# Four products ahead of a transpose, a constant column in a softmax, and new due times in a hand-planned kernel

## The chip, the core and the metric

The kernel runs on one core of one Trainium2 chip. The metric is the device time of one execution in microseconds (us); the times given are medians of a few executions. TensorE multiplies matrices, VectorE (DVE) and ScalarE (ACT) work elementwise and read its results from PSUM, GpSimd (POOL) works elementwise on SBUF, and SyncE (SP) issues the loads and stores.

## The reference, cut to what matters

Three stages follow each other: local and summary attention over 2 x 768 tokens with 8 heads of 64, a gated pair of products, and a second one with a clipped gate. All is float32, the weights arrive as float64.

```python
k_sum = k.reshape(B, H, nb, block, D).max(axis=3)       # block 32
v_sum = v.reshape(B, H, nb, block, D).mean(axis=3)
scores_all = concat([where(|i - j| < 16, q k^T / 8, -1e9), q k_sum^T / 8 + log(32)])
a = exp(scores_all - max(scores_all))
a = a / (sum(a) + 1e-09)
x = a @ concat([v, v_sum])
h = ((x @ w1) * (x @ w2)) @ w3 @ w_out                  # first block
g = (h @ w_in); g = g * clip(g + 3, 0, 6) / 6
out = g @ w_out2                                        # second block
```

## The kernel before

**Arithmetic.** Large products run with each operand split in a high and a low float32r part, and three products of 128 x 128 by 128 x 512 per term (PASSES, L338; the matmul is L347). The weights' 64-bit values are turned into float32 by hand (`to_f32`, L252: two ACT steps or an ACT and a DVE step, then a DVE step), then split by `to_hi_lo` (L298: ACT rounds the high part at L301, POOL or DVE subtracts at L304). `LO_DVE` lists the numbers of those conversions in `convert` whose subtraction goes to DVE instead of POOL; `convert` is called 40 times.

**Attention.** Twelve pairs of query tiles of 64 run in turn. `probabilities` (L450) makes the scores of both tiles of a pair (x = 0, 1; L483, plain float32 products on quarters of the array) into banks 6 and 7 of PSUM, scales and masks them on DVE into `sc` (L493), takes the maximum (DVE, L507), subtracts it (POOL, L509), exponentiates (ACT, L510), sums, adds 1e-9 and inverts (DVE, L513 to L515), and multiplies (POOL, L519). `attend` (L521) transposes the probabilities on TensorE (L529, four per x, x = 0 into bank 6, x = 1 into bank 7), copies them to `pt` (L536 on ACT for x = 0, L534 on DVE for x = 1), and multiplies by the values (L544). The order is scores of pair 0, scores of pair 1, transposes of pair 0, and so on. `con` holds the masks (480 columns) and an identity (128). Block sums and maxima come first: `first_k` (L384, three loads of 512 KB and a maximum each, L364), `first_v` (L392, the same with sums, L400), and `vsum_rows` (L421), which transposes the sums through bank 7 and copies them with ACT (L431).

**W'.** Beside the first four pairs, TensorE forms the product of two weights, `wprime` (L657), in 192 products; then come the blocks `ab` and `acc1` of the first stage, and from L900 on the second stage.

**The order.** Nothing is queued by hand. Every operation is entered in `Graph` with an engine, an estimated duration, a due time, what it reads and what it writes. `schedule` (L95) goes back from the users: an operation's due time is the smallest of its users' due times less its own duration and a latency; only TensorE operations bring a due time of their own:

```python
due = [o[2] if o[0] == "pe" else self.LAST for o in self.ops]
...
due[i] = min(due[i], due[u] - self.ops[i][1] - self.LAT.get(e, 40))
```

It then plays the engines forward, each taking of its ready operations the one due first, and the instructions are emitted in that planned order, so each engine's queue has it. The constants at L157 to L172 (DUE_..., LO_DVE, HOLD, OUT_AT and others) are the due times and options that the plan starts from. The two operations of a pair's transposes are entered as

```python
for x in range(2):
    g.op("pe", 480, due + 7 * us, lambda x=x: trans(x), [("s", i2, x), "con"], [("bank", bk[x])])
    ...
    g.op("dve" if x else "act", 690 if x else 600, due + 7.5 * us, fn, [("bank", bk[x])], [("pt", x)])
```

Of the kernel before, what the change touches and what calls it, by code (L numbers as in the profile page):

```python
# [63 lines left out]
class Graph:  # L64
# [7 lines left out]
    LAST = 1e9  # L72

    def __init__(self):
        self.ops = []
        self.writer, self.readers = {}, {}

    def op(self, eng, ns, due, fn, reads=(), writes=(), lock=False, slack=0, begin=0):
# [75 lines left out]

DUE_W = ((77.78, -6.43), (102.28, 1.95))  # L157
DUE_K, DUE_V, DUE_ROWS = 121.82, -109.4, 7.92
DUE_Q = (307.31, 41.78)
V_AT = 1  # L160
LO_DVE = [2, 9, 15, 16, 17, 18, 22, 26, 28, 29, 30, 31, 32, 36, 38, 42, 44, 45, 47]
L3_ACT = [2, 3, 4, 5, 6, 7, 8, 10, 11, 12, 15, 17, 18, 20, 22, 23, 24]
DUE_FF = 30.71
AHEAD, BEHIND = -16.03, -118.65
SUMS_AT, SUMS_DUE = 3, 5.0
POOL_MAX = ()
HOLD = 3512.7
SUMS_LATER = 22839.1
OUT_LATER = 31254.19
IN_AT = (8, 12)  # L170
LAST_ORDER = (0, 1, 4, 5, 2, 3, 6, 7)
OUT_AT, OUT_STEP = 174.13, 5.88  # L172


def build(tc, qd, kw, vw, kt, vt, consts, wp_in, w12_in, w2_in, out):
# [30 lines left out]
    kall = [att.tile([P, NPAIR, KS], F32, name=f"kall{i}") for i in range(2)]  # L206
    vall = [att.tile([P, DM], F32, name=f"vall{i}") for i in range(4)]
    qst = [att.tile([P, 2, NPAIR, QT], F32, name=f"qst{i}") for i in range(2)]
    sc = [att.tile([P, 2, NPAIR, NK], F32, name=f"sc{i}") for i in range(2)]
    pt = [att.tile([P, NPAIR * P], F32, name=f"pt{i}") for i in range(2)]  # L210
    st = [att.tile([P, 3, 2 * NPAIR], F32, name=f"st{i}") for i in range(2)]
    con = att.tile([P, 4 * NK + P], F32, name="con")
# [143 lines left out]

    load(0, lambda: con, consts, P * (4 * NK + P) * 4, ["con"])
    g.op("pool", 60, 0, lambda: nc.gpsimd.memset(three, 3.0), (), ["three"])


    def max32(due, x, c, reads):
# [88 lines left out]
    def probabilities(u, due, bk):  # L450
        i2, uu = u % 2, u % PPB
        ki, si, sti, qs = kall[i2], sc[i2], st[i2], qst[i2]
        vi = [2 * i2, 2 * i2 + 1]
        load(due - 5 * us, lambda: qs, qd[u], P * 2048, [("qs", i2)])
        near = u < PPK
        if near:
            lo = u * 2 * QT
            from_k = ["ksum"] + [
                ("kres", c) for c in range(3)
                if c * S // 3 + (WIN if c else 0) < lo + KW and lo < (c + 1) * S // 3 + WIN * (1 + (c == 2))]  # L460
        else:
            load(due - 5 * us, lambda: ki[:, :, NSUM : NSUM + KW], kw[u], P * KW * 16, [("kw", i2)])
            from_k = [("kw", i2), ("ks", i2, 0), ("ks", i2, KS - NSUM)]
        for h in range(2):
            rows = slice(0, NWIN) if h else slice(NSUM, NK)
            load(due - 4 * us, lambda h=h, rows=rows: vall[vi[h]][rows, :], vw[2 * u + h], NWIN * 2048, [("vw", vi[h])])

        def parts(x):
            if not near:
                lo = x * (KS - NK)  # L470
                return [(0, ki[:, :, lo : lo + NK])]
            lo = (2 * u + x) * QT
            return [(0 if x else NSUM, kres[:, :, lo : lo + NWIN]), (NWIN if x else 0, ksum)]

        def scores():
            for p in range(NPAIR):
                for n in range(2 if near else 1):
                    for x in range(2):
                        c, keys = parts(x)[n]
                        for h in range(2):  # L480
                            pr, o = slice(h * D, (h + 1) * D), (h + x) % 2 * D
                            rhs = keys[pr, p, :]
                            nc.tensor.matmul(  # L483
                                out=bank[bk[x]][o : o + D, p * NK + c : p * NK + c + rhs.shape[-1]],
                                lhsT=qs[pr, x, p, :], rhs=rhs, start=True, stop=True,
                            )

        g.op("pe", 1500 if near else 1100, due, scores, from_k + [("qs", i2)], [("bank", b) for b in bk])
        for x in range(2):
            m = (0 if uu == 0 else 1) if x == 0 else (3 if uu == PPB - 1 else 2)  # L490
            g.op(
                "dve", 660, due + 1 * us,
                lambda x=x, m=m: nc.vector.scalar_tensor_tensor(  # L493
                    out=si[:, x], in0=bank[bk[x]][:, 0 : NPAIR * NK].rearrange("p (a n) -> p a n", a=NPAIR),
                    scalar=SCALE, in1=con[:, m * NK : (m + 1) * NK].unsqueeze(1).to_broadcast((P, NPAIR, NK)),
                    op0=ALU.mult, op1=ALU.add,
                ), [("bank", bk[x]), "con"], [("s", i2, x)],
            )
        s8 = si.rearrange("p x a n -> p (x a) n")
        s1 = si.rearrange("p x a n -> p (x a n)")  # L500
        skeys = [("s", i2, 0), ("s", i2, 1)]

        def wide(k):
            return sti[:, k, :].unsqueeze(2).to_broadcast((P, 2 * NPAIR, NK))

        g.op("dve", 1160, due + 2 * us,
             lambda: nc.vector.tensor_reduce(out=sti[:, 0, :], in_=s8, op=ALU.max, axis=AX.X), skeys, [("st", i2)])  # L507
        g.op("pool", 2000, due + 3 * us,
             lambda: nc.gpsimd.tensor_tensor(out=s8, in0=s8, in1=wide(0), op=ALU.subtract), [("st", i2)], skeys)  # L509
        g.op("act", 1020, due + 4 * us, lambda: nc.scalar.activation(out=s1, in_=s1, func=AF.Exp), [], skeys)  # L510

        def inv():
            nc.vector.tensor_reduce(out=sti[:, 2, :], in_=s8, op=ALU.add, axis=AX.X)  # L513
            nc.vector.tensor_scalar(out=sti[:, 0, :], in0=sti[:, 2, :], scalar1=1e-9, scalar2=None, op0=ALU.add)
            nc.vector.reciprocal(out=sti[:, 1, :], in_=sti[:, 0, :])  # L515

        g.op("dve", 1560, due + 5 * us, inv, skeys, [("st", i2)])
        g.op("pool", 2000, due + 5.5 * us,
             lambda: nc.gpsimd.tensor_tensor(out=s8, in0=s8, in1=wide(1), op=ALU.mult), [("st", i2)], skeys)  # L519

    def attend(u, due, b0, b1):  # L521
        i2 = u % 2
        j, col = u // PPK, (u % PPK) * 2 * QT
        s0 = A_X + NPAIR * j
        si, vi, bk = sc[i2], [2 * i2, 2 * i2 + 1], (b0, b1)

        def trans(x):
            for p in range(NPAIR):
                nc.tensor.transpose(bank[bk[x]][0:NK, p * P : (p + 1) * P], si[:, x, p, :], ident)  # L529

        for x in range(2):
            g.op("pe", 480, due + 7 * us, lambda x=x: trans(x), [("s", i2, x), "con"], [("bank", bk[x])])
            if x:
                fn = lambda: nc.vector.tensor_copy(pt[1][0:NK, :], bank[bk[1]][0:NK, :])  # L534
            else:
                fn = lambda: nc.scalar.activation(out=pt[0][0:NK, :], in_=bank[bk[0]][0:NK, :], func=AF.Copy)  # L536
            g.op("dve" if x else "act", 690 if x else 600, due + 7.5 * us, fn, [("bank", bk[x])], [("pt", x)])

        def pv():
            for p in range(NPAIR):  # L540
                for x in range(2):
                    for h in range(2):
                        o = p * P + (h + x) % 2 * D
                        nc.tensor.matmul(  # L544
                            out=bank[b0][h * D : (h + 1) * D, p * P + x * QT : p * P + (x + 1) * QT],
                            lhsT=vall[vi[x]][0:NK, (2 * p + h) * D : (2 * p + h + 1) * D],
                            rhs=pt[x][0:NK, o : o + QT], start=True, stop=True,
                        )

        g.op("pe", 1100, due + 8 * us, pv, [("pt", x) for x in range(2)] + [(n, v) for n in ("vw", "vs") for v in vi],  # L550
             [("bank", b0)])
        xb = bank[b0].rearrange("p (a n) -> p a n", a=NPAIR)
        xh = ar[:, s0 : s0 + NPAIR, 0, col : col + 2 * QT]
        xl = ar[:, s0 : s0 + NPAIR, 1, col : col + 2 * QT]
        keys = [("t", s0 + p, h, col) for p in range(NPAIR) for h in range(2)]
        whole = [k for p in range(NPAIR) for k in both(s0 + p)]
        g.op("act", 600, due + 9 * us, lambda: nc.scalar.activation(out=xh, in_=xb, func=AF.Copy),
             [("bank", b0)] + whole, [k for k in keys if k[2] == 0])
        g.op(
            "dve", 690, due + 9.5 * us,  # L560
            lambda: nc.vector.tensor_tensor(out=xl, in0=xb, in1=xh.bitcast(F32), op=ALU.subtract),
            [("bank", b0)] + whole + [k for k in keys if k[2] == 0], [k for k in keys if k[2] == 1],
        )
# [117 lines left out]
    with tc.manual_schedule():  # L681
# [334 lines left out]
        for n, store, i, hh, bks, start in LAST:  # L1016
# [30 lines left out]
            for m in range(2):  # L1047
# [18 lines left out]
                elif n == 3:  # L1066
                    pair_out(due, 1, m, bks[m], 2 + m)
        for _, i in g.schedule():
            g.ops[i][3]()
        for cm in reversed(pools):  # L1070
            cm.__exit__(None, None, None)
# [71 lines left out]
```

## Time and profile before

| | before |
|---|---|
| median of 3 runs | 557.11 us |
| the runs | 555.17, 557.11, 557.39 us |
| the profiled execution, its own time | 555.27 us |
| its span on the core | 553.5 us |
| TensorE busy | 526.9 us |
| DVE busy | 375.7 us |
| ACT busy | 303.5 us |
| POOL busy | 289.2 us |

The span is the stretch from the first to the last instruction on the core; the 1.8 us around it belong to the execution's own time. Busy time alone doesn't tell what sets the end: TensorE's idle time, what ended it, and the chain of work that ended last do. Times in the rows below are counted from the start of the span.

### The profile page before, as it was taken

To read this page: it belongs to the slowest core of one execution; us is meant where nothing else is said; L and a number is where in the kernel's file an instruction comes from. 1 tells how busy PE (TensorE), PEld (TensorE's weight loads), DVE (VectorE), ACT (ScalarE), POOL (GpSimd) and SP (SyncE) were. 2 spreads that over 40 slices of the span, in tenths; PEclk is the share of its full clock that TensorE was granted. 3 is DMA by queue.
4 is the path that set the end of the run, shared out by engine and by line. 5 is a ranking of instruction groups with operands and counts; after the bars stand their busy time and mean duration, and the time that the engine had idled before them with its cause. 6 is when DMAs were issued, how large, how long until landed. Compare 5 with 4: busy or idle time off the path is not lost.

```text
span 553.5 us, 8514 instructions
## 1 busy us (share of the span) xinstructions
PE 526.9 (95%) x3112; PEld 431.4 (78%) x3112; DVE 375.7 (68%) x460; ACT 303.5 (55%) x517; POOL 289.2 (52%) x239
## 2 busy tenths in 40 slices
PE   0399999999999999999999999999999999999997
PEld 0388788888788888888888888888888887888875
DVE  5889978578463447777553866577775569689941
ACT  0879876484232446564545786655663456734630
POOL 0668454673221334374728665875785563644630
PEclk9789999999999999999999999999999999999999
DMA  8999678662241368633347576475444679877631
GB/s 318 363 364 336 197 245 261 187 195 62 65 123 53 121 215 270 218 115 115 114 157 229 222 247 209 156 263 172 150 174 142 209 264 366 294 256 231 190 103 75
DMA packets 54513, 111.32 MB, mean 201 GB/s; under 512 B 4792, under 2 KB 26296, under 8 KB 54472
## 3 DMA queue, kind: packets, MB, share of 16 engines
q1 hardware_dynamic: 54472, 110.79, 59.9%
q8 instruction: 24, 0.39, 0.3%
q14 instruction: 17, 0.14, 0.1%
HBM read 84.26 MB, written 26.21 MB: 200 GB/s over the span
## 4 chain that ended last, share of the span: by engine, by line
PE 91%; DMA 4%; DVE 1%; SPq 1%; POOL 1%; issue 0%; ACT 0%; ACTq 0%; DVEq 0%
PE bank L347 84%; PE bank L544 2%; PE bank L483 2%; PE bank L529 2%; DMA con<-in_con_dram 2%; DMA ws<-arena 1%; DMA w<-wo 1%; SPq L249 1%; DMA gj<-tg 1%; DVE sc L493 0%; POOL sc L519 0%; POOL sc L509 0%; SPq L1034 0%; PE bank L426 0%; DVE st L507 0%
## 5 line engine op out<-in xcount | busy, mean ns | idle before, releaser
L347 PE MATMUL bank<-arena,w 128*128 128x512 f32 x1152 | 268.3, 390 | 1.2 <-ACT late_f L855 1.2
L347 PEld LDWEIGHTS bank<-arena,w 128*128 128x128 f32 x1152 | 215.4, 188 | 47.2 <-ACT late_f L855 2.4
L347 PE MATMUL bank<-arena 128*128 128x512 f32 x960 | 230.9, 394 | 0.0
L347 PEld LDWEIGHTS bank<-arena 128*128 128x128 f32 x960 | 178.8, 189 | 38.2 <-issue 0.8
L292 DVE SCALAR_TENSOR_TENSOR c<-c,raw 128x512 uint32<-128x512 uint32 x48 | 47.7, 1006 | 22.2 <-ACT raw L283 17.5
L301 ACT ACTIVATE arena<-late_f 128x512 fp32r<-128x512 f32 x64 | 39.5, 628 | 39.2 <-DVE late_f L770 16.8
L304 POOL TENSOR_TENSOR w<-c,w 128x512 fp32r<-128x512 f32 x29 | 44.0, 1525 | 24.4 <-ACT w L301 24.3
L304 DVE TENSOR_TENSOR arena<-late_f,arena 128x512 fp32r<-128x512 f32 x44 | 39.6, 901 | 20.5 <-ACT arena L301 20.2
L826 POOL TENSOR_TENSOR late_f<-arena 128x512 f32<-128x512 f32 x16 | 23.2, 1447 | 44.7 <-DMA arena<-wo 30.4
L304 POOL TENSOR_TENSOR arena<-late_f,arena 128x512 fp32r<-128x512 f32 x20 | 29.5, 1476 | 32.0 <-ACT arena L301 26.5
L277 ACT ACTIVATE c<-raw 128x512 f32<-128x512 f32 x48 | 31.6, 663 | 25.2 <-DMA raw<-in_w_dram 24.3
L283 ACT ACTIVATE raw<-raw 128x512 uint32<-128x512 uint32 (+1 forms) x66 | 42.9, 655 | 0.0
L598 DVE TENSOR_TENSOR tg<-ta,bank 128x512 f32<-128x512 f32 x24 | 16.5, 685 | 38.8 <-PE bank L347 33.0
L304 POOL TENSOR_TENSOR raw<-c,raw 128x512 fp32r<-128x512 f32 x16 | 21.7, 1360 | 40.3 <-ACT raw L301 38.8
L509 POOL TENSOR_TENSOR sc<-sc,st 128x960 f32<-128x960 f32 x12 | 23.5, 1957 | 31.5 <-DVE st L507 31.5
L579 DVE TENSOR_TENSOR arena<-tg,arena 128x512 fp32r<-128x512 f32 x36 | 34.4, 955 | 5.4 <-ACT arena L574 4.8
L304 POOL TENSOR_TENSOR arena<-c,arena 128x512 fp32r<-128x512 f32 (+1 forms) x22 | 27.0, 1243 | 20.6 <-ACT arena L301 20.5
L574 ACT ACTIVATE arena<-tg 128x512 fp32r<-128x512 f32 x40 | 25.2, 629 | 20.1 <-DVE tg L598 16.6
L874 DVE SCALAR_TENSOR_TENSOR late_f<-ta,late_f 128x512 f32<-128x512 f32 x24 | 28.9, 1204 | 6.7 <-ACT ta L871 6.3
L770 DVE TENSOR_TENSOR late_f<-arena,late_f 128x512 f32<-128x512 f32 x24 | 29.1, 1242 | 6.2 <-DMA arena<-gj 6.1
L301 ACT ACTIVATE w<-c 128x512 fp32r<-128x512 f32 x40 | 24.6, 625 | 14.8 <-POOL c L770 6.5
L519 POOL TENSOR_TENSOR sc<-sc,st 128x960 f32<-128x960 f32 x12 | 22.0, 1832 | 17.0 <-DVE st L515 16.6
(68 smaller groups left out, 553.4 us busy)
## 6 DMA issues: line engine op xcount, KB each, us to landing
raw<-in_w_dram SPq DMA_DIRECT2D x48, 512.0 KB, 4.7
raw<-in_wp_dram SPq DMA_DIRECT2D x22, 512.0 KB, 6.0
wo<-raw SPq DMA_DIRECT2D x16, 512.0 KB, 3.4
arena<-wo SPq DMA_DIRECT2D x16, 512.0 KB, 3.3
ws<-arena SPq DMA_DIRECT2D x16, 512.0 KB, 3.4
w<-ws SPq DMA_DIRECT2D x32, 256.0 KB, 4.0
arena<-gj SPq DMA_DIRECT2D x24, 256.0 KB, 4.5
w<-wo SPq DMA_DIRECT2D x24, 256.0 KB, 4.0
```

The costliest lines, as they stand in the source:

```text
L277: lambda uf=uf, wf=wf: nc.scalar.activation(out=uf, in_=wf[:, :, 1], func=AF.Prelu, scale=2.0**-112, alpha=-(2.0**32)),
L283: lambda lw=lw: nc.scalar.activation(out=lw, in_=lw, func=AF.Copy, scale=2.0**-29 * (1 - eps), bias=7.5 * eps - 0.5),
L292: lambda ci=ci, ui=ui, lw=lw: nc.vector.scalar_tensor_tensor(out=ci, in0=ui, scalar=3, in1=lw, op0=ALU.logical_shift_left, op1=ALU.bitwise ...
L301: lambda: nc.scalar.activation(out=hi(), in_=src(), func=AF.Copy), keys, khi)
L304: lambda: e.tensor_tensor(out=lo(), in0=src(), in1=hi().bitcast(F32), op=ALU.subtract),
L347: nc.tensor.matmul(out=out_ap, lhsT=lhs(a), rhs=rhs(c), start=start and n == 0, stop=stop and n == 3 * len(terms) - 1, skip_group_check=skip,)
L509: lambda: nc.gpsimd.tensor_tensor(out=s8, in0=s8, in1=wide(0), op=ALU.subtract), [("st", i2)], skeys)
L574: g.op("act", 630, due, lambda: nc.scalar.activation(out=slot(s)[:, 0, :], in_=src_ap, func=AF.Copy), [src_key], [("t", s, 0)])
L579: lambda: eng.tensor_tensor(out=slot(s)[:, 1, :], in0=src_ap, in1=slot(s)[:, 0, :].bitcast(F32), op=ALU.subtract), [src_key, ("t", s, 0)], ...
L770: lambda: e.tensor_tensor(out=out(), in0=a(), in1=b(), op=op), [ka, kb], [ko], True)
L826: lambda i=i, s=s: nc.gpsimd.tensor_tensor(out=tmps[6 + i], in0=f32s(s, 0)(), in1=f32s(s, 1)(), op=ALU.add), both(s), [k])
L874: lambda: nc.vector.scalar_tensor_tensor(out=dst(), in0=t, scalar=6.0, in1=h(), op0=ALU.min, op1=ALU.mult),
```

## The change

Three things are changed. First, `attend` of pair 0 registers `kept_busy` under the number of the next operation entered, which is the transposition of half x = 0; when that operation is emitted, four float32 products of the identity and the 480 mask columns are emitted just ahead of it, into bank 6, which the transposes overwrite. They are no operation of the graph, so the plan has no time for them. Second, `sc` has one more column per row, set to 1e-9 once at the start; the sum is taken over that column too, and the addition falls away. Third, due times and options of the plan are set anew.

```diff
     def __init__(self):
-        self.ops = []
+        self.ops, self.before = [], {}
...
-DUE_W = ((77.78, -6.43), (102.28, 1.95))
-DUE_K, DUE_V, DUE_ROWS = 121.82, -109.4, 7.92
-DUE_Q = (307.31, 41.78)
+DUE_W = ((77.78, -6.43), (139.42, 1.95))
+DUE_K, DUE_V, DUE_ROWS = 121.82, -109.4, -31.56
+DUE_Q = (309.83, 41.78)
 V_AT = 1
-LO_DVE = [2, 9, 15, 16, 17, 18, 22, 26, 28, 29, 30, 31, 32, 36, 38, 42, 44, 45, 47]
+LO_DVE = [9, 13, 16, 17, 18, 22, 26, 28, 29, 30, 31, 32, 38, 42, 44, 47]
...
-DUE_FF = 30.71
-AHEAD, BEHIND = -16.03, -118.65
+DUE_FF = 31.07
+AHEAD, BEHIND = -15.06, -118.65
...
-HOLD = 3512.7
+N_BUSY = 4
+HOLD = 3470.14
...
-OUT_LATER = 31254.19
+OUT_LATER = 33015.51
...
-OUT_AT, OUT_STEP = 174.13, 5.88
+OUT_AT, OUT_STEP = 174.69, 5.88
...
-    sc = [att.tile([P, 2, NPAIR, NK], F32, name=f"sc{i}") for i in range(2)]
+    sc = [att.tile([P, 2, NPAIR, NK + 1], F32, name=f"sc{i}") for i in range(2)]
...
+    for i in range(2):
+        g.op("pool", 60, 0,
+             lambda i=i: nc.gpsimd.memset(sc[i].rearrange("p x a n -> p (x a) n")[:, :, NK : NK + 1], 1e-9),
+             (), [("s", i, x) for x in range(2)])
...
-        s8 = si.rearrange("p x a n -> p (x a) n")
-        s1 = si.rearrange("p x a n -> p (x a n)")
+        all8 = si.rearrange("p x a n -> p (x a) n")
+        s8 = all8[:, :, 0:NK]
...
-        g.op("act", 1020, due + 4 * us, lambda: nc.scalar.activation(out=s1, in_=s1, func=AF.Exp), [], skeys)
+        g.op("act", 1020, due + 4 * us, lambda: nc.scalar.activation(out=s8, in_=s8, func=AF.Exp), [], skeys)
...
-            nc.vector.tensor_reduce(out=sti[:, 2, :], in_=s8, op=ALU.add, axis=AX.X)
-            nc.vector.tensor_scalar(out=sti[:, 0, :], in0=sti[:, 2, :], scalar1=1e-9, scalar2=None, op0=ALU.add)
-            nc.vector.reciprocal(out=sti[:, 1, :], in_=sti[:, 0, :])
+            nc.vector.tensor_reduce(out=sti[:, 2, :], in_=all8, op=ALU.add, axis=AX.X)
+            nc.vector.reciprocal(out=sti[:, 1, :], in_=sti[:, 2, :])
-        g.op("dve", 1560, due + 5 * us, inv, skeys, [("st", i2)])
+        g.op("dve", 1420, due + 5 * us, inv, skeys, [("st", i2)])
...
+    def kept_busy():
+        for _ in range(N_BUSY):
+            nc.tensor.matmul(out=bank[6][:, 0 : 4 * NK], lhsT=ident, rhs=con[:, 0 : 4 * NK], start=True, stop=True)
...
+        if u == 0:
+            g.before[len(g.ops)] = kept_busy
         for x in range(2):
             g.op("pe", 480, due + 7 * us, lambda x=x: trans(x), [("s", i2, x), "con"], [("bank", bk[x])])
...
         for _, i in g.schedule():
+            g.before.get(i, lambda: None)()
             g.ops[i][3]()
```

## Rows read from the trace of the kernel before

**Rows 1.** Busy time of each engine, with share of the span and instructions.

```profile
PE 526.9 (95%) x3112; PEld 431.4 (78%) x3112; DVE 375.7 (68%) x460; ACT 303.5 (55%) x517; POOL 289.2 (52%) x239
```

**Rows 2.** TensorE's waits: line, what ended them, total us, times, longest us.

```profile
PE bank L426 <- DMA con<-in_con_dram: 13.1, 1, 13.1
PE bank L529 <- POOL sc L519: 7.0, 1, 7.0
...
PE bank L347 <- ACT late_f L855: 1.2, 1, 1.2
```

**Rows 3.** Chain that ended last, in order of time: start us, us, what.

```profile
4.27 8.65 DMA con<-in_con_dram
...
14.10 0.60 ACT vall L431
...
14.74 2.24 PE bank L483 x34
...
20.16 1.14 DVE sc L493 x2
...
26.84 1.97 PE bank L529 x8
28.80 2.27 PE bank L347 x6
31.08 1.08 PE bank L544 x32
...
71.72 32.89 PE bank L347 x144
...
239.94 201.52 PE bank L347 x888
```

**Rows 4.** Stretches: length, busy us (instructions) by engine, granted clock, DMA share, GB/s.

```profile
20.36:30.60 10.24, 3.76 (x13) 3.38 (x14) 9.51 (x15) 9.27 (x18) 8.92 (x8) 0.50 0.99 358
...
30.00:31.00 1.00, 1.00 (x4) 0.55 (x2) 1.00 (x1) 1.00 (x2) 0.87 (x2) 0.70 1.08 442
...
37.27:38.15 0.88, 0.88 (x9) 0.88 (x8) 0.88 (x2) 0.56 (x1) 0.88 (x1) 1.00 1.09 424
```

**Rows 5.** Timelines of DVE, ACT and TensorE: start us, us, instruction, idle before it.

```profile
28.22 0.68 DVE L534 COPY pt<-bank 120x512 f32<-120x512 f32 x1
...
28.84 0.60 ACT L536 ACTIVATE pt<-bank 120x512 f32<-120x512 f32 x1 [0.97 <-PE bank L529]
...
67.48 0.62 PE L529 MATMUL bank<-con,sc 128*120 128x128 f32 x4
...
68.42 0.68 DVE L534 COPY pt<-bank 120x512 f32<-120x512 f32 x1
...
68.64 0.60 PE L529 MATMUL bank<-con,sc 128*120 128x128 f32 x4
```

**Rows 6.** Stretches of L483 alone: length, PE and PEld busy (records), granted clock, DMA.

```profile
14.74:17.00 2.26, 2.26 (x60) 2.21 (x60) 1.00 1.05 406
18.37:19.65 1.28, 1.28 (x64) 1.28 (x64) 1.00 1.00 389
34.42:35.67 1.25, 1.25 (x64) 1.15 (x64) 1.00 1.12 243
126.19:127.17 0.98, 0.98 (x32) 0.75 (x32) 1.00 0.19 44
```

**Rows 7.** Timelines of SP (issues) and DVE: the last loads and maximum of k.

```profile
2.98 1.24 SPq L249 DMA_DIRECT2D kres<-in_kt_dram  x2
...
12.17 1.22 DVE L364 TENSOR_REDUCE ksum<-kres 128x32 f32<-128x1024 f32 x1 [0.25 <-DMA kres<-in_kt_dram]
```

**Rows 8.** Timelines of DVE and GpSimd around the end of the first pair's probabilities.

```profile
24.16 0.20 DVE L514 TENSOR_SCALAR st<-st 128x8 f32<-128x8 f32 x1
...
24.40 0.20 DVE L515 RECIPROCAL st<-st 128x8 f32<-128x8 f32 x1
...
24.30 0.74 POOL L304 TENSOR_TENSOR arena<-c,arena 128x256 fp32r<-128x256 f32 x1
...
24.99 1.79 POOL L519 TENSOR_TENSOR sc<-sc,st 128x960 f32<-128x960 f32 x1
```

More of the change, by code (lines that the diff above doesn't have):

```diff
@@ L493, in probabilities @@
                 lambda x=x, m=m: nc.vector.scalar_tensor_tensor(
-                    out=si[:, x], in0=bank[bk[x]][:, 0 : NPAIR * NK].rearrange("p (a n) -> p a n", a=NPAIR),
+                    out=si[:, x, :, 0:NK], in0=bank[bk[x]][:, 0 : NPAIR * NK].rearrange("p (a n) -> p a n", a=NPAIR),
                     scalar=SCALE, in1=con[:, m * NK : (m + 1) * NK].unsqueeze(1).to_broadcast((P, NPAIR, NK)),
@@ L528, in trans @@
             for p in range(NPAIR):
-                nc.tensor.transpose(bank[bk[x]][0:NK, p * P : (p + 1) * P], si[:, x, p, :], ident)
+                nc.tensor.transpose(bank[bk[x]][0:NK, p * P : (p + 1) * P], si[:, x, p, 0:NK], ident)
+        if u == 0:
+            g.before[len(g.ops)] = kept_busy
         for x in range(2):
```

## The prediction

> **What bounds the kernel now.** I read the shares of busy time first, then who TensorE waited for, then the chain of work that ended last, and the clock by stretches last. TensorE is busy 526.9 of 553.5 us [rows 1]. What it waits for stands in three rows [rows 2]: 13.1 us for the constants' load at the start, 7.0 us for the product on GpSimd that finishes the first pair's probabilities (L519), and 1.2 us far behind, for ScalarE. From 26.84 us on the chain is TensorE alone, one piece behind the other, up to the end of a piece of 201.52 us at 441.5 [rows 3]. Whatever is put on TensorE's queue behind 26.84 us therefore moves the end by its own length, and whatever is put into the 7.0 us before it costs nothing. That is the question of this change: on which side do the four products fall?
>
> The clock matters as well. From 20.36 to 30.60 us TensorE is granted 0.50 of its clock (1.2 GHz), and 0.70 on average in the 31st microsecond; before the fall it had idled since the second pair's scores, and before the rise it had run transposes and products for some 3.8 us [rows 4]. The eight transposes of the first pair take 1.97 us in this stretch, those of the second pair at the full clock 0.88 us; six products take 2.27 us, where the piece of 144 in 32.89 us gives 0.228 us each, so 1.37 us for six [rows 3, 4]. The low clock costs 1.10 + 0.90 = 2.0 us there.
>
> **The place of the four products.** They are emitted ahead of the graph's operation for half x = 0 of the first pair's transposes. But the halves do not run in that order. DVE copies half x = 1 (L534), ACT half x = 0 (L536). In the first pair DVE's copy starts at 28.22 us, while the eight transposes run until 28.80, and ACT's starts at 28.84, after 0.97 us of waiting for TensorE [rows 5]. The fourth pair, whose halves stand apart, shows the same: four transposes at 67.48, DVE's copy at 68.42, and only at 68.64 the other four [rows 5]. So x = 1 goes first, and the code says why: a transpose's due time is that of its copy, DVE's copy is rated 690 ns and ACT's 600, so x = 1 is due 90 ns earlier, and both become ready together, when L519 ends. Nothing in the diff touches these two ratings. The products then stand **between the two halves**, behind the wait for L519. They cover none of the 7.0 us, and they delay half x = 0, its copy and everything behind it on TensorE.
>
> **Their price.** A float32 product with a full 128 x 128 stationary side and 480 columns is not in the trace. Each float32 product of the code leaves two records (16 products at L544, 32 records). The lower end: two passes at the rate of the long piece, 2 x 0.228 x 480/512 = 0.43 us, so 1.7 us for four [rows 3]. The upper end: L544, 16 products of 64 columns in 1.08 us; if two run at once on the two halves of the columns, that is 0.135 us for 64 columns and 1.01 us for 480, so 4.1 us for four [rows 3]. In between lie the scores at full clock: 16 products of 120 columns in 0.98 us, or 16 of 96 and 16 of 24 in 1.25 us [rows 6]. If four run at once on the quarters, these are 0.245 us for one set of 120 columns and 0.3125 us for two sets of 120 together; the difference, 0.0675, is the fixed part of a set, and 0.1775 us goes with 120 columns. That is 4 x 0.1775 + 0.0675 = 0.78 us for 480 columns and **3.1 us for four**. I take this, since it alone separates columns from fixed parts; 1.7 and 4.1 stay for the range. The Trainium skill, "FP8 and Floating Point Precision", section "TensorE Precision Notes", says that true float32 takes four passes; the estimate by it is 16 passes of 0.214 us, 3.4 us, and the sum would be 558.4 us.
>
> That is the price at full clock. The products begin in the half-clock stretch and take about twice as long there, but then they stand in it in place of the four transposes and the six products that paid for it before; as long as the clock rises as long after TensorE's return as it did, the low clock costs the same 2.0 us, and the change adds 3.1 us.
>
> **The earlier rows.** DUE_ROWS falls from 7.92 to -31.56. Before, the sums' transposes (L426) were due just ahead of the first scores, because both use bank 7. Now their inputs come first on SP's queue: the three v loads and the constants ahead of the k loads. In the trace the last two k loads are issued at 2.98 us, the constants at 4.27 us, landing at 12.92 [rows 3, 7]. DVE began the maximum of the last k load at 12.17 us, when it had landed, so the constants took 0.75 us of the queue behind it. With them ahead, that maximum (1.22 us [rows 7]) ends at 12.17 + 0.75 + 1.22 = 14.1 us, and the scores start there. They started at 14.74 us, behind the ACT copy of 14.10 to 14.70, which will then be long done [rows 3]; a few of them had slipped in before that copy, 0.15 us of work. The gain is some 0.4 us; were the k load not later, it would be 0.75 us more. Against it: with the sums' transposes gone from 13 us, TensorE has worked for a shorter time when the second scores come; their 64 records took 1.28 us against 2.26 us for 60 of the first set [rows 6], so they can lose 1 us, part of it hidden by DVE. I take -0.3 us, with -1.2 and +1.0 as ends.
>
> **The guard.** The sum now runs over 121 columns and the addition (L514, 0.20 us) falls away twelve times. In the first pair the reciprocal ended at 24.60 us, and L519 started at 24.99 because GpSimd was in a subtraction (L304) from 24.30 for 0.74 us [rows 8]; so 0.20 us are hidden, and nothing is gained on the path. In the other eleven pairs TensorE does not wait. The 8 more columns, the strided rows and two 8-column fills at the start cost nothing, hidden by the same waits; without that cover they are hundredths of a microsecond.
>
> **The new dues.** Due times of other engines than TensorE are not read by the planner, so OUT_LATER has no effect. DUE_W, DUE_Q and AHEAD give TensorE operations due times that lie behind those of their users, which take precedence. DUE_FF shifts all of these together. HOLD and OUT_AT move loads of the last part by half a microsecond of planning. Of LO_DVE only the entries under 40 are read (there are 40 such conversions): 2, 15 and 36 go to GpSimd and 13 comes to DVE. GpSimd is busy 52% and DVE 68% [rows 1], so this costs nothing on average; the third conversion's subtraction can stand in front of the second pair's L519, and that pair's transposes came late enough (37.27 us) to hide it. For a flipped order I leave 1 us either way, around the 1.2 us wait [rows 2].
>
> **The sum.** On the profiled execution: 555.27 + 3.1 - 0.3 = 558.1 us. This execution lies 1.84 us under the median of the runs; the four known executions (555.17, 555.27, 557.11, 557.39) have a mean of 556.2, and I forecast from that: 556.2 + 2.8 = **559.0 us**, 0.3% over the median of 557.11. About 0.5%, 2.8 us, is what a measurement can tell from no change: under 554.3 counts as faster, over 559.9 as slower.
>
> **Rivals.**
> *The products stand in front of both halves.* Then they start when DVE frees bank 6, after the first of the two steps from 20.16 us [rows 3], so at some 20.7 us, inside the wait, cost nothing, and TensorE comes to the transposes at the full clock: -2.0 - 0.3 from 556.2, 553.9 us, faster. The wait of 7.0 us speaks for it [rows 2], the order of the two copies against it [rows 5]. The Trainium skill, "TensorE: Matmul & The Clock Gate", section "Part 4: PE-mode transpose", says that the full clock does not engage for transposes, by which only the six products would gain 0.9 us and this rival would end at 555.0 us; the trace disagrees, 0.88 us at granted 1.00 against 1.97 us at 0.50. Chance 0.10.
> *Between the halves, but cheap,* at the lower price, or with the clock rising sooner than before: 556.2 + 1.7 - 0.3 = 557.6 us, or, if that gives a whole microsecond back, 556.6 us. No change. Chance 0.18.
> *Between the halves, and the clock stays low through them* (slower). The place is the stretch from the first four transposes to the end of the products: if no rise comes inside it, they cost twice 3.1, and the sum is 556.2 + 6.2 - 0.3 = 562.1 us. It decides from the moment the rise comes after the products' end. Against it: the first scores, float32 products too, were followed by scores at double the pace [rows 6]. Chance 0.12.
>
> **How the numbers follow.** The forecast has 0.60; its own spread, 557.4 to 560.5 us, puts 0.18 of that over 559.9. Faster 0.08 (the first rival, less its upper edge), slower 0.18 + 0.12 = 0.30, same 0.62. The range from 556.2 to 561.2 us leaves out most of the first rival and the upper half of the third, under 0.2.
>
> **What the profile after would show.** Right: eight records of 480 columns between 26 and 33 us, behind the first wait for L519 and ahead of ACT's first copy, which waits 4 us or more for TensorE; L544 of the first pair starting near 33.5 instead of 31.08 us; the L426 piece near 9 us. Wrong: the eight records at 20.7 us and a granted clock of 1.00 at the transposes (first rival); L544 before 32.5 us (second); 0.50 throughout the records (third). A wait of TensorE beyond 31 us other than the 1.2 us one would be an order that I have not foreseen.

## The result: slower by 1.0%

The changed kernel takes 561.88 us (median of 6 runs, 560.60 to 563.30), the one before 556.70 (6 runs, 555.17 to 557.39). The ratio is 1.0100, with a 95% interval of 1.0078 to 1.0122: 5.6 us slower, where 559.0 was forecast and the range ended at 561.2. The profiled execution took 563.11 us, with a span of 561.3, so it is one of the longer ones, as the profiled one of before (555.27) was one of the shorter.

The busy times after (to [rows 1]):

```profile
PE 532.0 (95%) x3120; PEld 432.8 (77%) x3120; DVE 369.9 (66%) x446; ACT 302.1 (54%) x517; POOL 290.3 (52%) x243
```

TensorE has 5.1 us more work. That alone comes near the loss by the runs, but between these two executions the span grew by 7.8 us, so it also idles longer. Its waits after (line, what ended them, total us, times, longest us; to [rows 2]):

```profile
PE bank L431 <- DVE vsum L405: 8.8, 1, 8.8
PE bank L537 <- POOL sc L523: 7.8, 2, 6.8
PE bank L488 <- DMA qst<-in_q_dram: 6.0, 2, 3.8
PE bank L348 <- ACT late_f L865: 1.6, 1, 1.6
PE bank L537 <- DVE sc L498: 0.8, 1, 0.8
PE bank L554 <- DVE pt L544: 0.4, 1, 0.4
PE bank L348 <- ACT ta L606: 0.2, 1, 0.2
```

The line numbers have moved: L537 are the transposes (L529 before), L523 the product on GpSimd ahead of them (L519), L488 the scores (L483), L554 the values product (L544), L348 the large products (L347), L431 the transposes of the sums (L426), and L527 are the four new products. The wait of 6.8 us for L523 is still there, so the products did not fill it. New are 1.0 us more for L523, 0.8 and 0.4 us, all of them near 230 to 243 us, far from the products. At the start little is different in sum: 8.8 and 6.0 us where there were 13.1, 1.3 and 0.2. All waits together are 25.6 us against 22.8.

The chain after (start us, us, what; to [rows 3]):

```profile
27.52 1.11 PE bank L537 x4
28.63 4.66 PE bank L527 x8
33.29 0.44 PE bank L537 x4
33.73 1.40 PE bank L348 x6
35.12 1.08 PE bank L554 x32
...
216.84 4.49 DMA wo<-raw
...
221.81 5.31 DMA wo<-raw
...
227.19 4.75 DMA raw<-in_w_dram
...
236.97 1.80 POOL sc L514
...
241.41 1.77 POOL sc L523
...
243.22 1.09 PE bank L537 x8
...
247.44 207.41 PE bank L348 x914
```

Two things are to be seen. The products stand between the halves: four transposes, eight records, four transposes. The first pair's values product starts at 35.12 us instead of 31.08, 4.04 us later: 0.68 us because L523 ends later, and 1.11 + 4.66 + 0.44 + 1.40 = 7.61 us from there on where it was 1.97 + 2.27 = 4.24 us [rows 3], so 3.37 us for the products. And where the chain before was TensorE alone up to 441.5 us, it now leaves TensorE at 211 us for a stretch of stores, a weight load and the probabilities of the last pair, before it comes back to TensorE at 243 us.

The copies after, from the timelines of DVE and ACT (to [rows 5]):

```profile
28.80 0.68 DVE L544 COPY pt<-bank 120x512 f32<-120x512 f32 x1
...
33.76 0.60 ACT L546 ACTIVATE pt<-bank 120x512 f32<-120x512 f32 x1 [5.41 <-PE bank L537]
```

DVE copies its half at 28.80 us, before the products are through; ACT waits 5.41 us for the half behind them.

### The profile page after: what moved, and what is told of

Its sections match the earlier page's. It is cut to its first block, busy times and chain, and to the rows that moved or that the text cites. A ratio compares the mean times of both kernels' runs of the same rounds, so it can differ in the third digit from the quotient of the medians.

```text
span 561.3 us, 8521 instructions
## 1 busy us (share of the span) xinstructions
PE 532.0 (95%) x3120; PEld 432.8 (77%) x3120; DVE 369.9 (66%) x446; ACT 302.1 (54%) x517; POOL 290.3 (52%) x243
## 4 chain that ended last, share of the span: by engine, by line
PE 84%; DMA 9%; POOL 2%; ACT 2%; DVE 1%; issue 1%; SPq 1%; POOLq 0%; ACTq 0%
PE bank L348 77%; DMA raw<-in_w_dram 2%; PE bank L488 2%; PE bank L537 2%; DMA wo<-raw 2%; PE bank L554 2%; DMA kres<-in_kt_dram 1%; DMA qst<-in_q_dram 1%; DMA ws<-arena 1%; DMA w<-wo 1%; POOL sc L514 1%; PE bank L527 1%; POOL sc L523 1%; DVE st L512 1%; ACT raw L284 1%
## 5 line engine op out<-in xcount | busy, mean ns | idle before, releaser
L348 PE MATMUL bank<-arena,w 128*128 128x512 f32 x1152 | 267.8, 390 | 1.6 <-ACT late_f L865 1.6
L348 PEld LDWEIGHTS bank<-arena,w 128*128 128x128 f32 x1152 | 215.6, 188 | 47.8 <-ACT late_f L865 2.8
L348 PE MATMUL bank<-arena 128*128 128x512 f32 x960 | 231.3, 394 | 0.2 <-ACT ta L606 0.2
L348 PEld LDWEIGHTS bank<-arena 128*128 128x128 f32 x960 | 177.6, 188 | 38.3 <-issue 1.1
L293 DVE SCALAR_TENSOR_TENSOR c<-c,raw 128x512 uint32<-128x512 uint32 x48 | 46.9, 989 | 27.6 <-ACT raw L284 22.8
L305 DVE TENSOR_TENSOR arena<-late_f,arena 128x512 fp32r<-128x512 f32 x44 | 41.4, 943 | 19.4 <-ACT arena L302 19.2
L514 POOL TENSOR_TENSOR sc<-sc,st 128x960 f32<-128x960 f32 x12 | 23.5, 1956 | 40.0 <-DVE st L512 38.2
L305 POOL TENSOR_TENSOR arena<-c,arena 128x512 fp32r<-128x512 f32 (+1 forms) x23 | 27.9, 1226 | 22.8 <-ACT arena L302 22.8
L606 ACT ACTIVATE ta<-bank 128x512 f32<-128x512 f32 x24 | 14.2, 591 | 31.0 <-PE bank L348 31.0
```

What stands on the lines that cost most here:

```text
L293: lambda ci=ci, ui=ui, lw=lw: nc.vector.scalar_tensor_tensor(out=ci, in0=ui, scalar=3, in1=lw, op0=ALU.logical_shift_left, op1=ALU.bitwise ...
L305: lambda: e.tensor_tensor(out=lo(), in0=src(), in1=hi().bitcast(F32), op=ALU.subtract),
L348: nc.tensor.matmul(out=out_ap, lhsT=lhs(a), rhs=rhs(c), start=start and n == 0, stop=stop and n == 3 * len(terms) - 1, skip_group_check=skip,)
```

## The experiments

Each kernel ran on the chip beside the kernel before. The table gives the ratio to the runs of before that stood beside it, and the ratios, not the medians, are what to compare; 0.001 is 0.56 us.

| kernel | ratio | 95% interval | median us |
|---|---|---|---|
| changed kernel | 1.0100 | 1.0078 to 1.0122 | 561.88 |
| changed, no products (e1) | 1.0042 | 1.0023 to 1.0060 | 559.17 |
| before + products between the halves (e2) | 1.0059 | 1.0039 to 1.0079 | 559.53 |
| changed, products in front of both (e3) | 1.0015 | 0.9997 to 1.0034 | 557.37 |
| before + products in front of both (e4) | 0.9972 | 0.9952 to 0.9993 | 555.43 |
| before + AHEAD (e5) | 0.9997 | 0.9977 to 1.0017 | 556.33 |
| before + guard column (e6) | 1.0017 | 0.9997 to 1.0038 | 557.79 |
| before + DUE_ROWS (e7) | 1.0011 | 0.9996 to 1.0026 | 557.04 |
| before + OUT_AT (e8) | 1.0130 | 1.0103 to 1.0156 | 564.14 |
| changed, OUT_AT back (e9) | 1.0062 | 1.0041 to 1.0084 | 560.01 |
| changed, OUT_AT back, products in front (e10) | 0.9972 | 0.9947 to 0.9997 | 555.67 |
| before + eight products between (e11) | 1.0111 | 1.0087 to 1.0135 | 563.25 |
| before + two products in front (e12) | 0.9992 | 0.9971 to 1.0014 | 556.51 |
| before + OUT_AT and AHEAD (e13) | 1.0056 | 1.0035 to 1.0078 | 559.45 |
| changed, AHEAD back (e14) | 1.0125 | 1.0091 to 1.0159 | 564.27 |

**The changed kernel without its products (e1).**

```diff
-N_BUSY = 4
+N_BUSY = 0
```

> The changed kernel without its four products. Theory A: they are the whole loss. In the trace after they take 4.66 us, of which 0.5 us at the other half's transposes and 0.9 us at six products come back through the risen clock: so about 3.2 us net, and this kernel runs in the time of before, 556.7 us, or a few tenths under it. Theory B: the new dues cost some 2 us by themselves, through the waits for pair 11's probabilities (0.8 + 1.0 + 0.4 us in the trace after, none there before): then 558.5 to 559 us, and those waits are still there.

Measured: 1.0042, 2.3 us slower than before (1.3 to 3.3). Theory B holds: something else in the change costs some 2 us. The new waits are still there, 0.9 us (DVE) at 228.00 and 0.7 us (POOL) at 238.62 us in the trace.

**The products alone (e2).** The patch is that of the change, in the kernel before: `kept_busy` registered under the number of half x = 0.

> The kernel before, with the four products between the halves of the first pair's transposes and nothing else. Theory A: the whole 5 us, so 561.5 to 562 us. Theory B: 4.66 us of products less 1.4 us given back by the clock, 3.2 us, so 559.9 us.

Measured: 1.0059, 3.3 us. Theory B again. The two parts, 0.42% and 0.59%, make the whole 1.00%. Near 230 us this kernel's TensorE waits for nothing.

**The products in front of both halves (e3, e4).** The products are registered under the number of half x = 1, which runs first.

```diff
-        if u == 0:
-            g.before[len(g.ops)] = kept_busy
         for x in range(2):
+            if u == 0 and x == 1:
+                g.before[len(g.ops)] = kept_busy
```

> The changed kernel with the four products moved in front of both halves. If the place is the fault, they run from some 20.8 us on (when DVE frees bank 6) inside the wait for L523 and cost nothing, and both halves and the six products behind them run at full clock: the first pair's values product would start at 27.5 + 0.87 + 1.4 = 29.8 instead of 35.1 us, 5.3 us earlier, 556.6 us. If the clock falls again in the rest of the wait, the products are still hidden but nothing is gained by them: 2 us more, 558.6 us.

> The kernel before with the four products in front of both halves and nothing else: the first rival of the prediction as a kernel. If the clock holds until the transposes, 1.1 + 0.9 = 2.0 us off, 554.7 us. If it falls again between the products and the transposes, 556.7 us. If transposes gain nothing by the clock, 555.8 us.

Measured: 1.0015 and 0.9972. TensorE's timeline of e4 (start us, us, instruction, idle before it):

```profile
20.91 4.93 PE L524 MATMUL bank<-con 128*128 128x480 f32 x8 [0.64 <-DVE sc L494]
26.97 1.09 PE L534 MATMUL bank<-con,sc 128*120 128x128 f32 x8 [1.14 <-POOL sc L520]
27.81 1.64 PE L348 MATMUL bank<-arena 128*128 128x512 f32 x6
```

The products start when DVE frees bank 6, at 20.91 us, and fill all but 1.14 us of the wait. The eight transposes take 1.09 us from the first start to the last end where the profiled execution of before had 1.97, and the six products 1.64 where it had 2.62. So the place is the fault of the products, not the products. The gain is 1.6 us, near the 2.0 us by which the low clock was costed, and the place moves the changed kernel by 0.85%, 4.7 us. The prediction had weighed a rule of the Trainium skill ("TensorE: Matmul & The Clock Gate", section "Part 4: PE-mode transpose"), that the full clock does not engage for transposes. The trace disagrees: behind the products they run at the full clock, 1.09 us. The time alone can't decide it, its interval runs from 0.4 to 2.7 us of gain, and whether transposes by themselves bring the clock up no run shows.

**Two products in front instead of four (e12).** `N_BUSY = 2` in e4.

> The kernel before with two products in front of both halves: they run from 20.9 to about 24 us, and TensorE then idles for some 3 us until the transposes. If what counts is that TensorE has worked at all in the wait, the clock is high at the transposes and the time is that with four, 555.4 us. If it has to have worked up to the transposes, the clock is low again: transposes in 1.9 us, six products in 2.3 to 2.9, 556.4 us, as before.

Measured: 0.9992, no change. TensorE's timeline of e12:

```profile
20.12 3.57 PE L524 MATMUL bank<-con 128*128 128x480 f32 x4 [0.89 <-DVE sc L494]
26.19 1.96 PE L534 MATMUL bank<-con,sc 128*120 128x128 f32 x8 [2.50 <-POOL sc L520]
27.80 2.53 PE L348 MATMUL bank<-arena 128*128 128x512 f32 x6
```

and two stretches of it (length, PE busy, granted clock, DMA share, GB/s):

```profile
22.00:23.00 1.00, 1.00 (x3) 0.50 0.97 385
...
26.00:27.00 1.00, 0.81 (x4) 0.50 1.02 397
```

The clock was low through the two products and stayed low; the transposes take 1.96 us again. What is bought in the wait is not work but the clock at its end, and two products did not buy it. The longer gap behind them (2.50 us against 1.14) is not the reason: the granted clock was still 0.50 when the second product ended.

**The price of a product (e11).** `N_BUSY = 8` in e2.

> The kernel before with eight products between the halves instead of four: the second four run at the full clock, so their price stands free of the clock. By the prediction's 0.78 us each: 559.5 + 3.1 = 562.6 us, and 0.39 us between starts of the records in the trace. By the lower end, 0.43 us each: 561.2 us. If the second four are partly hidden by a wait behind them (the copies or the conversions), less than that.

Measured: 1.0111 against 1.0059 with four, so 0.52%, 2.9 us for the second four by the ratios, with some 1.7 us either way. TensorE's timeline, two consecutive cuts of it:

```profile
33.49 1.37 PE L524 MATMUL bank<-con 128*128 128x480 f32 x3
...
33.89 1.37 PE L524 MATMUL bank<-con 128*128 128x480 f32 x3
```

The records start 0.40 us apart, so a product (two records) takes 0.80 us at the full clock and four take 3.2 us. The prediction's 0.78 us, from the scores, holds; the lower and the upper end (0.43 and 1.01) don't. It is the records that decide this, the times leave both ends open. The way to the 0.78 (four products at once on the quarters, a fixed part for each set) was not tested, only what came of it. By the four passes that the Trainium skill states ("FP8 and Floating Point Precision", section "TensorE Precision Notes") and this kernel's float32r rate the estimate was 0.86 us, near it from the other side.

**The dues one by one (e5 to e8).** DUE_FF, HOLD, and DUE_W, DUE_Q and OUT_LATER leave every engine's order as it was when they are set alone, so they were not run. LO_DVE does change the order and was not run alone; it is in e9 and e10 with the rest. The others:

```diff
-AHEAD, BEHIND = -16.03, -118.65      # e5
+AHEAD, BEHIND = -15.06, -118.65
-DUE_K, DUE_V, DUE_ROWS = 121.82, -109.4, 7.92      # e7
+DUE_K, DUE_V, DUE_ROWS = 121.82, -109.4, -31.56
-OUT_AT, OUT_STEP = 174.13, 5.88      # e8
+OUT_AT, OUT_STEP = 174.69, 5.88
```

e6 has the guard column of the change and nothing else.

> The kernel before with AHEAD alone set to its new value. The prediction held that this due time is overridden by that of its users; but with it alone the transposes of several later pairs stand elsewhere among the products on TensorE's queue. Theory: TensorE is the bound and only the order differs, so 556.4 us, no change, and no new wait near 230 us. Rival: the pairs' transposes are now asked for before their probabilities are there, and this makes the new waits of the changed kernel (0.8 + 1.0 us before the transposes near 230 and 240 us): 558.2 us.

> The kernel before with the guard column alone (the addition gone, sums over 121 columns, the plan's 1420 ns). The prediction's step: nothing on the path, 556.4 us. Rival: the shorter plan flips orders of loads and stores late in the kernel; then a wait that was not there before and up to 2 us more, 558.4 us.

> The kernel before with DUE_ROWS alone set to its new value, so that the constants and the v loads come before the k loads. The prediction's step: -0.3 us, between -1.2 and +1.0. From the traces of the changed kernel: the second scores wait for their q load (2.2 us, up to 18.4 us) as they also do in two runs of the old order (1.3 and 1.5 us), and run at the low clock in both; so no change, 556.4 us. Rival: the low clock at the first pair's values product, as in the changed kernel without products (1.77 instead of 1.08 us), comes from this order: +0.7 us, 557.1 us.

> The kernel before with OUT_AT alone set to its new value: stores and loads of the last weights change places on SP's queue, and nothing on TensorE's. Theory: this makes the new waits of the changed kernel near 230 and 240 us, where two stores (wo<-raw, 4.5 and 5.3 us) and a weight load stand in the chain ahead of pair 11's probabilities: 0.8 + 1.0 us, 558.2 us. Rival: the order on SP is worth nothing here, 556.4 us, and the waits come from AHEAD or the guard.

Measured: 0.9997, 1.0017 and 1.0011, none of them clear of no change, and 1.0130 for OUT_AT: 7.2 us from 0.56 us of a planning time. Its wait on TensorE (start us, us, instruction, idle before it):

```profile
234.32 1.93 PE L529 MATMUL bank<-con,sc 128*120 128x128 f32 x8 [4.70 <-DVE sc L493]
```

and the chain that leads there:

```profile
215.83 6.36 DMA wo<-raw
...
223.11 7.39 DMA raw<-in_w_dram
...
230.52 0.66 ACT c L277
231.18 0.55 ACT raw L283
...
231.75 0.69 DVE c L292
232.44 0.60 DVE tg L598
233.04 1.14 DVE sc L493 x2
...
236.25 4.74 PE bank L347 x12
```

OUT_AT is the planned time from which the last weights' loads may start. With it half a microsecond later the plan has another order on SP's queue. SP's timeline in e8:

```profile
205.83 0.38 SPq L249 DMA_DIRECT2D raw<-in_w_dram  x1
214.47 0.80 SPq L249 DMA_DIRECT2D vall<-in_vw_dram  x2
215.36 0.38 SPq L249 DMA_DIRECT2D raw<-in_w_dram  x1
215.83 0.38 SPq L318 DMA_DIRECT2D wo<-raw  x1
222.25 0.33 SPq L249 DMA_DIRECT2D raw<-in_w_dram  x1
...
223.11 6.70 SPq L249 DMA_DIRECT2D raw<-in_w_dram  x2
```

and in the kernel before:

```profile
208.47 0.32 SPq L318 DMA_DIRECT2D wo<-raw  x1
211.49 0.81 SPq L249 DMA_DIRECT2D raw<-in_w_dram  x2
212.46 0.80 SPq L249 DMA_DIRECT2D vall<-in_vw_dram  x2
216.03 0.34 SPq L318 DMA_DIRECT2D wo<-raw  x1
216.42 3.50 SPq L249 DMA_DIRECT2D raw<-in_w_dram  x2
```

Before, a store of converted weights (wo) leaves at 208.47 us, two weight loads follow at 211.49, and the last pair's two value loads (vall) come behind them. In e8 the value loads stand in front. Their buffer is read by the tenth pair's values product (L544), so they can leave only behind it, and SP stands for 8.3 us until then, against 0.3 us before. The store, which does not need that product, waits along and leaves at 215.83. The four raw buffers are used in turn, and the next load into the store's buffer waits 6.4 us more, until 222.25. What stands behind it on the queue is late too, among it the load of 223.11 us that ends the chain's waiting at 230.50. (The trace of e8 is 2.0 us behind at the start of this stretch: the eleventh pair's scores start at 205.81 us, 203.80 before. That leaves 5.4 of the store's 7.4 us for the order.) SP's wait for this values product is 7.3 to 8.3 us in all six kept traces with the new OUT_AT, 0.3 to 1.6 us in the ten with the old one, and new waits of TensorE between 220 and 245 us stand in those six alone.

The conversions that wait for the late load stand at the head of ACT's and DVE's queues (L277, L283, L292), and the masking of the last pair's scores (L493), which needs no weight at all, stands behind them on DVE. The eleventh pair's transposes write into the two banks that the masking still has to read. So a late load of weights which nobody needs yet becomes a wait of TensorE. And the wait costs more than its 4.70 us, because the clock has fallen by its end (length, busy us by engine, granted clock, DMA share, GB/s):

```profile
234.32:236.25 1.93, 1.93 (x9) 1.93 (x10) 0.16 (x1) 1.74 (x4) 0.64 (x1) 0.50 0.05 19
```

The eight transposes take 1.93 instead of 0.88 us [rows 4], and the twelve products behind them 4.74 us, where twelve took 2.73 at this place before. With the wait that makes 7.8 us; 7.2 was measured (5.7 to 8.7).

**OUT_AT set back in the changed kernel (e9, e10).**

> The changed kernel with OUT_AT alone set back to 174.13, the products still between the halves. Theory: OUT_AT's order of stores and loads on SP's queue is what the new dues cost; the waits of 0.8 + 0.4 + 1.0 us near 230 and 240 us go, and what is left of the loss are the products: 561.9 - 2.3 = 559.6 us. Rival: the loss beside the products lies in DUE_ROWS, LO_DVE and the guard together, each too small to see alone: 561.5 us or more, though the waits go.

> The changed kernel with OUT_AT set back and the products in front of both halves. If both faults add, 557.4 us less the 1.0 us of waits near 230 us in the trace with the products in front, less the fifth of a microsecond before it: 556.2 us; with the whole 2.3 us of theory back, 555.1 us, as the kernel before with the products in front (555.4 us).

Measured: 1.0062, the ratio of the products alone (1.0059), and 0.9972, that of the products in front alone. The waits near 230 us are gone in both; e9's TensorE waits for L523 once:

```profile
PE bank L537 <- POOL sc L523: 6.8, 1, 6.8
```

So OUT_AT is what the change cost beside the products (2.1 us between the changed kernel and e9, with 1.7 us either way), and DUE_ROWS, LO_DVE, AHEAD and the guard together cost nothing that can be measured, with some 1.6 to 1.8 us either way. e10 is faster than both kernels, as is e4; between these two the runs can't decide.

**Why OUT_AT costs 2.3 us in the changed kernel and 7.2 alone (e13, e14).**

> The kernel before with OUT_AT and AHEAD set to their new values. Theory: with AHEAD the loads of the eleventh and twelfth pair come one place earlier among the weight loads on SP's queue, so that OUT_AT costs less than alone: the rest of the changed kernel's loss, 2.3 us, so 558.9 us, with waits of 0.5 to 1 us each near 230 and 240 us instead of one of 4.7 us. Rival: the two don't touch each other and the smaller loss in the changed kernel comes from LO_DVE or the guard: 564 us as with OUT_AT alone.

> The changed kernel with AHEAD alone set back. Theory: OUT_AT then costs its whole 7 us instead of 2.3, with a wait of some 4 us or more near 235 us: 566.5 us. Rival: 562 us as the changed kernel.

Measured: 1.0056, so AHEAD takes 4.1 of OUT_AT's 7.2 us back in the kernel before, and 1.0125 in the changed kernel without AHEAD's new value, 1.4 us more than with it, where 4.6 were expected. TensorE's waits near 230 us in e13:

```profile
228.60 1.12 PE L529 MATMUL bank<-con,sc 128*120 128x128 f32 x8 [0.98 <-DVE sc L493]
...
239.25 1.09 PE L529 MATMUL bank<-con,sc 128*120 128x128 f32 x8 [0.70 <-POOL sc L519]
```

and in e14:

```profile
235.70 1.06 PE L537 MATMUL bank<-con,sc 128*120 128x128 f32 x8 [3.13 <-POOL raw L305]
```

With both dues there are two short waits, as in the changed kernel (0.77 and 1.04 us), and the transposes behind them run at the full clock; without AHEAD there is one long one. In e13 the first theory's amount and shape are met, but not by the way it named: the last pair's value loads stand at the same place on SP's queue as in e8, behind one weight load and ahead of the next and of the store. The trace shows another way: six products stand between the tenth pair's transposes and its values product, where e8 has twelve, so the buffer is read sooner and SP stands for 7.3 instead of 8.3 us. That this makes the whole 4.1 us is not shown. In e14 there is one wait again, but of 3.13 us where 4 or more was expected, the transposes behind it run at the full clock (1.06 us), and the amount is not met. Its interval, 1.0091 to 1.0159, also overlaps that of the changed kernel, so that AHEAD matters there is not shown; what the other dues take off was not tried.

## Why the prediction was wrong, step by step

**The place of the products** was right, and not by luck: it was read from two copies' order in the trace and from two ratings in the code. The trace after has the eight records between the halves, and e2, e3 and e4 show what the place is worth: 3.3 us between the halves, -1.6 us in front of both.

**The price** was right: 3.1 us forecast, 3.3 us measured by e2 (2.2 to 4.4), 3.2 by the records in e11. That the low clock costs about the same with products as without agrees with the one trace after: 3.37 us for products and clock together. The first pair's values product started at 35.12 us and not near 33.5, because the product on GpSimd ahead of it (L523) ended 0.68 us later in that execution, the products cost 3.37 us, not 3.1, and nothing came off for the rows. The prediction's 558.4 us for four passes is counted from the profiled execution; from 556.2 us, as the forecast is, it would be 559.3.

**The earlier rows** were sized at -0.3 us and gave nothing that the runs can show (e7, +0.6 us, -0.2 to +1.4). The loads did change places, and the first scores did come earlier: on average they end at 16.83 us in the nine kept traces of the old order and at 15.84 in the seven of the new. But I did not name what is late next. In the new order the second scores wait 2.15 to 2.24 us for their q load, and the first pair's transposes start at 27.15 us on average, where they had started at 27.08. The gain ended there. I wrote of three rows of waits; TensorE's waits of before have another of over a microsecond, ahead of these scores, and it pointed there:

```profile
PE bank L483 <- DVE sc L493: 1.3, 1, 1.3
```

**The guard** at nothing: e6 gives +0.9 us with an interval from -0.2 to +2.1, so no error that the runs can show.

**The new dues** are the step that failed. "HOLD and OUT_AT move loads of the last part by half a microsecond of planning", the prediction says, and it leaves 1 us either way for a flipped order. For HOLD even that is too much, it changes by 0.04 us and flips nothing. OUT_AT cost 7.2 us alone (e8) and some 2 us in the changed kernel (2.3 by e1, 2.1 by e9). The amount of a due time says nothing on what it costs; it costs what the flipped order costs. I had looked for gaps on TensorE, found one of 1.2 us, and put the uncertainty around it. The stretch that decided showed no gap in the trace before. What it did show, and I did not read, is that the last pairs' loads and probabilities share SP, ACT and DVE with the conversion of the last weights, which nothing hurries. The last sign of being wrong that I had named is the one that came: waits of TensorE beyond 31 us other than the 1.2 us one.

Of AHEAD I wrote that the users' due times take precedence. That holds for the scores, which I had followed; the transposes and values products are entered some 16 us ahead of the scores in due time, so theirs do count, and TensorE's order of several pairs changed. It is worth nothing alone (e5), but in the kernel before it takes 4.1 us off what OUT_AT costs (e13).

**The sum.** 556.2 + 3.1 - 0.3 = 559.0 us; with the rows' 0 and the 2.3 us that the dues cost by e1 it is 561.6, against 561.9 measured. The rivals were three ways of placing and pricing the products; a due time that reorders a queue was none of them, and the range had 1 us for it.

## What to carry to other kernels

Filler work belongs in front of the first instruction that waits, and which one that is must be read from the order on the engine, not from the order in the source; a helper that is tied to an operation's number follows that operation wherever the planner puts it. In a planned kernel a changed constant is to be costed by the queues that it reorders: list what changes places, and look at what stands behind each of it on every engine, above all behind a load or store that waits for a buffer. When a wait is shortened, name the next input that comes late before the gain is counted.

## What the runs showed of the hardware

**The clock at the end of a wait.** Four products in the wait of 7 us left TensorE at the full clock 1.14 us after the last of them (eight transposes in 1.09 us, e4); two products, the last of which ended 2.50 us before the transposes, left it at 0.50 throughout (1.96 us, e12). At the end of e8's wait of 4.70 us it was 0.50; behind the waits of 0.98 and 0.70 us in e13 the transposes ran at the full clock (1.12 and 1.09 us).

**A granted clock that the durations contradict.** In the changed kernel the profile gives 1.00 for the stretch in which the first four transposes took 1.11 us, where the other four took 0.44 (length, busy us by engine, granted clock, DMA share, GB/s):

```profile
27.00:28.00 1.00, 0.48 (x3) 0.48 (x4) 0.61 (x2) 1.00 (x3) 1.00 (x2) 1.00 1.06 393
```

The first scores of the kernel before show the same, 2.26 us at a granted 1.00 [rows 6], and e1's eight transposes take 1.96 us at a granted 1.00, as e12's do at 0.50. In the first 35 us of these executions the column missed low stretches; there the duration of a known instruction is the better witness.
